# Exponentials kept as 25-bit integers, and their low halves converted on three engines

## The chip, the cores and the metric

The kernel runs on one core of a Trainium2 chip. A core has five engines that run side by side, each through its own list of instructions in order: TensorE (PE; its weight loads are listed as PEld), VectorE (DVE), ScalarE (ACT), GpSimd (POOL) and SyncE (SP, which here only issues DMA transfers). They work on SBUF, the memory on the core with 128 partitions; PE writes its products to PSUM, a small memory that DVE and ACT read. They wait for each other through semaphores.

The metric is the device time of one execution in microseconds (us), as the median of the runs. The time of one instruction is given in nanoseconds (ns) where it is short.

## The reference

Attention over pooled queries, then a mixture of experts on its output. Cut to what matters here:

```python
def _attn_ref(q, k, v):                       # batch 8, heads 8, S 1152, D 64
    q_pool = q.reshape(B, H, S // 2, 2, D).mean(axis=3)
    scores = 1.0 / np.sqrt(D) * np.matmul(q_pool, k.transpose(0, 1, 3, 2))
    scores = scores - np.max(scores, axis=-1, keepdims=True)
    attn = np.exp(scores)
    attn = attn / (np.sum(attn, axis=-1, keepdims=True) + 1e-09)
    return np.matmul(attn, v)

def _moe_ref(x, modality_id, w_gate, modality_bias, w1, w2):   # 4608 tokens, 512, 8 experts, 1024
    logits = x @ w_gate + modality_bias[modality_id]
    e_idx = np.argmax(logits, axis=1)
    ...
    for e in range(E):
        mask = e_idx == e
        h = np.maximum(x[mask] @ w1[e], 0.0)
        out[mask] = gate_w[mask, None] * (h @ w2[e])
```

The experts are chosen by the largest logit, so attention's result is needed with nearly float32 precision: a rounding that changes the order of two logits sends a token to another expert.

## The kernel before

**Stages.** Attention runs over 32 pairs (`npairs`); a pair is one head of two neighbouring batches, so that 2 x 64 dimensions fill the 128 partitions. A pair has 18 steps (`NSTEP`). Its scores are computed in 18 chunks, 9 for each of the two heads (`j`), of 128 keys by 576 queries. The experts follow after the last pair; their routing is worked out beside the attention, in small DVE operations.

**High and low parts.** PE takes 32-bit data at a lower precision than float32, and 16-bit data exactly. So each operand is split into a rounded high part and what is left, and a product is the sum of three matmuls: high x high, high x low, low x high.

**A chunk, in order** (`scores`, lines 717 to 735):

- In two halves of 288 queries, two matmuls each write the scores, minus the row's maximum, to a PSUM tile `psc` of three buffers (lines 729, 730). The maximum comes in as one more row of the operand (`mr`, line 664), which also carries the logarithm of `PSC`, a constant factor on all exponentials.
- ACT takes the exponential to an SBUF tile `Pe` in float32 (line 731).
- The high part `Ph` costs no instruction: it is the upper 16 bits of each float32 of `Pe`, read as bfloat16 with a stride of four bytes.
- The low part `Pl`, in float16, is `Pe - Ph`: one operation with two inputs of 576 elements (line 735), one or two steps later. It runs on POOL, but for the chunks in `DVE_LO` (3 of 18), and for those in `DVE_LAST` (13) in the last pair, which run on DVE.

**Products with v** (`pv`, lines 752 to 765). For each of five groups of queries and each of the nine chunks there are three matmuls, `Ph` x `vh`, `Ph` x `vl` and `Pl` x `vh`, with `Ph` or `Pl` as the weights. `vh` (`VH`, float16, two buffers) is v scaled by a power of two and rounded, made by ACT in three parts (`values`, line 652); `vl` is what is left, made by DVE (line 650). A column of ones beside `vh` gives the sum of the exponentials, by which `evac` divides (lines 772 to 787).

**Beside it, for the next pairs.** DVE takes the row maxima of a first, rough pass over the scores: PE writes 27 tiles `pm` per pair (line 681) and DVE reduces each to one column `mp` (line 682). Keys and queries are split (ACT line 560, DVE lines 547 and 573, POOL line 541), and SP moves the parts into the matmuls' operands `B1`, `B2` and `QB` (line 510). Each pair loads its keys and queries (`load_kq`, line 523) and its values (`load_v`, line 527); the finished output of two pairs is stored by SP (line 197). ACT squares v for its scale (line 618); the scale is a short chain of DVE operations (lines 627 to 639) behind a matmul with a 128 x 128 tile `ones` (line 625).

**What sets the order.** Inside attention the order on PE and ACT is written out by hand: the loop at lines 918 to 948 goes through the steps, and in each of them through the letters of `ORD`. `s` is half a chunk of scores with its exponential, `M` and `X` a tile of the maximum pass, `V` six groups of products with v, and `F` what was put off to this step: `later(n, f)` puts off f by n steps, and `at(t, p, f)` sets it to step t of pair p. The `T_` constants at the top of the file are those steps: `T_VH` for `vh` and `T_VL` for `vl`, for instance. So the low part of an even chunk comes in the step after its exponential, that of an odd chunk in the step after that.

Small SBUF tiles of the routing (`route` and `place`, in pools with one buffer) have a name and a place each.

Of the kernel before, what the change touches and what calls it, by code (L numbers as in the profile page):

```python
# [31 lines left out]
KQ = S + SQ  # L32
NPAIR = BATCH // 2 * H
NKC = S // P
PSC = 64.0
NSTEP = 2 * NKC
NP = 18
T_LIST = -122
# [21 lines left out]
T_POW = 0  # L60
T_VH = (2, 2, 4)
T_VL = (7, 7, 8)
QH_DVE = True
HI_DVE = ()
EV_ACT = ()
# [3 lines left out]
DVE_LAST = (1, 2, 3, 4, 5, 7, 8, 10, 11, 13, 14, 16, 17)  # L69
T_G0 = 2  # L70
T_X0 = 11
DVE_LO = (0, 7, 15)


T = BATCH * SQ
# [59 lines left out]
class Router:  # L135
# [86 lines left out]
    def route(self, g, eng):  # L222

        nc, sm = self.nc, self.sm
        while self.added[g] < H // 2:
            yield 1
        lg = sm.tile([P, NT, E], F32, name="lg8")
        nc.vector.tensor_reduce(lg, self.lg[g].rearrange("p t (w e) -> p t e w", w=3), op=ALU.add, axis=AX.X)
        ts = slice(g * NT, (g + 1) * NT)
        bc = lambda a: a.unsqueeze(2).broadcast_to([P, NT, E])  # L230
        be = lambda a: a.unsqueeze(1).broadcast_to([P, NT, E])
        w = sm.tile([P, NT, E], F32, name="w_a")
        w2 = sm.tile([P, NT, E], F32, name="w_b")
        inv = sm.tile([P, NT], F32, name="inv")
        nc.vector.tensor_scalar(inv, self.mid[:, ts], -1.0, 1.0, op0=ALU.mult, op1=ALU.add)
        nc.vector.tensor_tensor(w, be(self.b0[:, 0]), bc(inv), op=ALU.mult)
        nc.vector.tensor_tensor(w2, be(self.b0[:, 1]), bc(self.mid[:, ts]), op=ALU.mult)
        yield RS
        nc.vector.tensor_tensor(w, w, w2, op=ALU.add)
        nc.vector.tensor_tensor(lg, lg, w, op=ALU.add)  # L240
        yield RS
        mx = sm.tile([P, NT], F32, name="mx")
        nc.vector.tensor_reduce(mx, lg, op=ALU.max, axis=AX.X)
        nc.vector.tensor_tensor(lg, lg, bc(mx), op=ALU.subtract)
        yield RS
        nc.scalar.activation(w, lg, AF.Exp)
        nc.vector.tensor_single_scalar(w2, lg, 0.0, op=ALU.is_ge)
        key = sm.tile([P, NT, E], F32, name="key")
        nc.vector.scalar_tensor_tensor(key, w2, -float(E), be(self.ie), op0=ALU.mult, op1=ALU.add)
        kmin = sm.tile([P, NT], F32, name="kmin")  # L250
        nc.vector.tensor_reduce(kmin, key, op=ALU.min, axis=AX.X)
        yield RS
        oh = sm.tile([P, NT, E], F32, name="oh")
        nc.vector.tensor_tensor(oh, key, bc(kmin), op=ALU.is_equal)
        oh16 = sm.tile([P, NT, E], BF16, name="oh16")
        nc.vector.tensor_copy(oh16, oh)
        nc.vector.tensor_single_scalar(self.exp[:, ts], kmin, float(E), op=ALU.add)
        yield RS
        sx = sm.tile([P, NT], F32, name="sx")
        nc.vector.tensor_reduce(sx, w, op=ALU.add, axis=AX.X)  # L260
        nc.vector.tensor_single_scalar(sx, sx, EPS, op=ALU.add)
        gt = sm.tile([P, NT, 2], F32, name="gt")
        for i in range(2):
            nc.vector.reciprocal(gt[:, :, i], sx)
        eng.dma_start(out=self.xs[g * NT * P:(g + 1) * NT * P, DM:XW].rearrange("(t p) d -> p t d", p=P), in_=gt)
        yield RS
        for _ in range(self.ll - 1):
            yield
        pr = self.pm(4)[:, 0:(NT + 1) * E].rearrange("p (t e) -> p t e", e=E)
        nc.tensor.matmul(pr[:, 0:NT], self.up, oh16, start=True, stop=False, skip_group_check=True)  # L270
        for s in range(NT):
            nc.tensor.matmul(pr[:, s + 1:], self.on, oh16[:, s:s + 1].broadcast_to([P, NT - s, E]), start=False, stop=s == NT - 1,
                             skip_group_check=True)
        pos = sm.tile([P, NT, E], F32, name="posw")
        nc.vector.tensor_tensor(pos, pr[:, 0:NT], be(self.base), op=ALU.add)
        nb = self.keep.tile([P, E], F32, name="base")
        nc.vector.tensor_tensor(nb, pr[:, NT], self.base, op=ALU.add)
        self.base = nb
        yield RS
        nc.vector.tensor_tensor(pos, pos, oh, op=ALU.mult)  # L280
        nc.vector.tensor_reduce(self.pos[:, ts], pos, op=ALU.add, axis=AX.X)
# [81 lines left out]
    def place(self, nt, late):  # L363
# [1 line left out]
        nc, sm = self.nc, self.sm  # L365
        be = lambda a: a.unsqueeze(1).broadcast_to([P, nt, E])
        yield
        oh = sm.tile([P, nt, E], F32, name=f"ohp{nt}")
        nc.vector.tensor_tensor(oh, self.exp[:, 0:nt].unsqueeze(2).broadcast_to([P, nt, E]), be(self.ie), op=ALU.is_equal)
        yield  # L370
        w = sm.tile([P, nt, E], F32, name=f"ohw{nt}")
        new = lambda name: sm.tile([P, NTT], F32, name=name)[:, 0:nt]

        def pick(o, of):
# [106 lines left out]
def attention(tc, ctx, att, ident, npairs, xpool, on_two, on_split, jobs, side, set_pm, started, ahead, hip):  # L481
# [14 lines left out]
    some = lambda i: ps_max.tile([P, 512], F32, name="pm") if i in IN_PM else small()  # L496
    set_pm(some)

    ones = const.tile([P, P], F32, name="ones")
    B2, QB, VH = [], [], []  # L500
    for i in range(2):
        B2.append(const.tile([D + 1, 2 * KQ], F32R, name=f"B2_{i}"))
        QB.append(const.tile([P, 9, P], F32R, name=f"QB_{i}"))
    for i in range(2):
        VH.append(const.tile([P, NKC, 2, D + 2], F16, name=f"VH_{i}"))

    st = {p: {} for p in range(npairs)}

# [112 lines left out]
    def power(p):  # L621

        s = st[p]
        pt = some(1)
        nc.tensor.matmul(pt[:, 0:NSQ], ones, s["ss"], start=True, stop=True)
        sq = sm.tile([P, 1], F32, name="sq", bufs=1)
        nc.vector.tensor_reduce(sq, pt[:, 0:NSQ], op=ALU.add, axis=AX.X)
        half = sm.tile([P, 1], I32, name="half", bufs=1)
        nc.vector.tensor_single_scalar(half, sq.bitcast(I32), 24, op=ALU.logical_shift_right)
        ex = sm.tile([P, 2], I32, name="ex", bufs=1)  # L630
        nc.vector.tensor_scalar(ex[:, 0:1], half, -1.0, 205.0, op0=ALU.mult, op1=ALU.add)
        nc.vector.tensor_scalar(ex[:, 1:2], half, 1.0, 49.0, op0=ALU.mult, op1=ALU.add)
        sc = sm.tile([P, 2], I32, name="sc")
        nc.vector.tensor_single_scalar(sc, ex, 23, op=ALU.logical_shift_left)
        s["sc"], s["isc"] = sc.bitcast(F32)[:, 0:1], sc.bitcast(F32)[:, 1:2]
        if p % 2 == 0:
            s["both"] = xpool.tile([P, 2], F32, name="both", bufs=3)
        r = slice(p % 2 * D, (p % 2 + 1) * D)
        nc.vector.tensor_copy(st[p - p % 2]["both"][r], sc.bitcast(F32)[r])
# [3 lines left out]
    def values(p, i, lo):  # L643

        s = st[p]
        c = slice(3 * i, 3 * i + 3)
        v = flat(s["v"].rearrange("p (c j d) -> p c j d", c=NKC, j=2)[:, c])
        vh = flat(VH[p % 2][:, c, :, 0:D])
        if lo:
            nc.vector.scalar_tensor_tensor(flat(s["vl"][:, c]), v, s["sc"], vh, op0=ALU.mult, op1=ALU.subtract)  # L650
        else:
            nc.scalar.activation(vh, v, AF.Copy, scale=s["sc"])

    def row(p, mp, u0, u1):

# [61 lines left out]
    def scores(p, j, c, n):  # L717
# [1 line left out]
        s = st[p]  # L719
        b1, b2 = s["B1"], B2[p % 2]  # L720
        ks = slice(j * S + c * P, j * S + (c + 1) * P)
        Pe = pP.tile([P, SQ], F32, name="Pe")
        Pl = pP.tile([P, SQ], F16, name="Pl")
        Ph = Pe.bitcast(BF16).rearrange("p (n w) -> p n w", w=2)[:, :, 1]
        s["P", j, c] = (Ph, Pl)
        for t in range(2):
            qs = slice(2 * S + j * SQ + t * 288, 2 * S + j * SQ + (t + 1) * 288)
# [3 lines left out]
            nc.scalar.activation(Pe[:, t * 288:(t + 1) * 288], pt, AF.Exp, scale=1.0 / 16)  # L731
            if t == 0:
                yield
        eng = nc.vector if (j * NKC + c) in (DVE_LAST if p == npairs - 1 else DVE_LO) else nc.gpsimd
        later(n, lambda: eng.tensor_tensor(Pl, Pe, Ph, op=ALU.subtract))  # L735

    def split_x(p, x2):

# [13 lines left out]
    def pv(p, j, x2):  # L752

        s = st[p]
        W = D + 2
        vh, vl = VH[p % 2], s["vl"]
        hs = slice((p % 2) * D, (p % 2 + 1) * D)
        tile_ = lambda: ps_pv.tile([P, 512], F32, name="xp", tag="pv")[:, 0:5 * W].rearrange("p (g w) -> p g w", w=W)

        def products(qs, out):  # L760
            for c in range(NKC):
                Ph, Pl = s["P", j, c]
                nc.tensor.matmul(out, Ph[:, qs], vh[:, c, j, 0:D + 1], start=c == 0, stop=False, skip_group_check=True)  # L763
                nc.tensor.matmul(out[:, 0:D], Ph[:, qs], vl[:, c, j], start=False, stop=False, skip_group_check=True)  # L764
                nc.tensor.matmul(out, Pl[:, qs], vh[:, c, j, 0:D + 1], start=False, stop=c == NKC - 1, skip_group_check=True)  # L765
                yield

        def evac(xp, g0, t0, n):

            rs = sm.tile([P, 5], F32, name="rs")[:, 0:n]  # L770
            rr = sm.tile([P, 5], F32, name="rr")[:, 0:n]
            nc.vector.tensor_scalar(rs, xp[:, g0:g0 + n, D], 1.0, EPS * PSC, op0=ALU.mult, op1=ALU.add)
            nc.vector.reciprocal(rr, rs)
            def done():
                if p % 2:
# [98 lines left out]
    nc.gpsimd.memset(ones, 1.0)  # L874
    for i in range(2):
        nc.gpsimd.memset(VH[i][:, :, :, D:D + 2], 1.0)
    nc.gpsimd.memset(B2[1][D:D + 1, 0:2 * S].bitcast(F32), 1.0)
    mxq.append(maxpass(0, mp0))
    advance(mxq, T_PRE)
# [2 lines left out]
    for p in range(npairs):  # L882
# [21 lines left out]
        go(T_POW + d, power)  # L904
        for i in range(3):
            go(T_VH[i] if p else min(T_VH[i] + d, NKC), values, i, False)
            go(T_VL[i] if p else min(T_VL[i] + d, NKC), values, i, True)
        for j in range(2):
            go(NKC * (j + 1) + LAG, lambda p, j: pvq.append(pv_task(p, j)), j, end=False)
# [442 lines left out]
```

## Time and profile before

| | us |
|---|---|
| median of three runs | 1434.89 |
| lowest and highest run | 1434.81, 1444.65 |
| the profiled execution | 1437.58 |
| its span, first to last instruction | 1435.8 |

The profile is that of one execution. The span is the time from the first to the last instruction on the core, and "busy" is the time in which an engine had an instruction under way. "Granted clock" is the share of full speed at which PE ran. Views of the profile used below:

- **Busy table by stages:** one row for each stretch of time (us from the start), with its length and, for each engine, the busy us and the number of instructions in brackets.
- **Waits:** an engine and line, what it waited for, the us in total, how many times, and the longest. PEld is PE's weight load. SPq is SP's queue of DMA issues.
- **Groups:** line, engine, operation, output <- input with partitions x elements and types, the count; then busy us in all, mean ns of one; then the engine's idle time just before them and what ended it.
- **Durations of one line:** the count, then the smallest, median and largest ns, and when the first and the last began.

### The profile page before, as it was taken

What the parts mean: (1) busy time and instruction counts of PE and PEld (TensorE: products, weight loads), DVE (VectorE), ACT (ScalarE), POOL (GpSimd) and SP (SyncE); (2) the same over time, 40 slices, a digit from 0 to 9 for tenths busy, and PEclk for the clock granted to TensorE, in tenths of its full rate; (3) what the DMA queues carried; (4) which work ended last, traced back from release to release, by engine and by line L of the source; (5) the groups of instructions that cost most, each with busy time, mean ns of one, the idle gap of its engine ahead of it and who ended that gap; (6) DMA issues with size and microseconds to landing.
All of it is one profiled execution on the core that took longest, in us unless ns stands there. A gap on an engine that the chain in (4) does not pass through costs nothing. (4 is left out here: it accounts for less than half of the span.)

```text
span 1435.8 us, 38561 instructions
## 1 busy us (share of the span) xinstructions
PE 1292.6 (90%) x14976; PEld 1181.7 (82%) x14976; DVE 1185.2 (83%) x2233; ACT 868.6 (60%) x2001; POOL 900.5 (63%) x684
## 2 busy tenths in 40 slices
PE   6899999889999988899998888997989899999995
PEld 4788888888888888888887877886879788989894
DVE  6899998889988999889899999956998566566572
ACT  3566776656666665666665556655555566666661
POOL 6667777757777776677775566736444365554642
PEclk9999999989999999999999999999999999999998
DMA  9668788769788786796886868638867778889791
GB/s 230 177 175 196 187 216 193 165 145 208 191 194 187 197 206 147 177 205 183 195 186 161 169 164 178 136 108 230 233 209 245 221 243 256 245 256 274 242 245 41
DMA packets 211284, 280.53 MB, mean 195 GB/s; under 512 B 92816, under 2 KB 150208, under 8 KB 207121
## 3 DMA queue, kind: packets, MB, share of 16 engines
q1 hardware_dynamic: 204960, 258.15, 72.2%
q0 software_dynamic: 6128, 19.78, 4.0%
q8 instruction: 122, 2.00, 0.6%
q14 instruction: 74, 0.60, 0.1%
HBM read 146.11 MB, written 19.18 MB: 115 GB/s over the span
## 5 line engine op out<-in xcount | busy, mean ns | idle before, releaser
L735 POOL TENSOR_TENSOR Pl<-Pe 128x576 f16<-128x576 f32 x470 | 593.3, 1279 | 278.5 <-ACT Pe L731 269.8
L731 ACT ACTIVATE Pe<-psc 128x288 f32<-128x288 f32 x1152 | 432.6, 409 | 293.2 <-PE psc L730 278.4
L682 DVE TENSOR_REDUCE mp<-pm 128x1 f32<-128x384 f32 x832 | 425.5, 542 | 53.0 <-PE pm L681 50.8
L681 PE MATMUL pm<-hi,QB 128*128 128x384 f32 x832 | 321.1, 386 | 59.2 <-DVE mp L682 55.6
L729 PE MATMUL psc<-B 128*128 128x288 f32 x1152 | 350.2, 311 | 19.6 <-ACT Pe L731 18.4
L730 PE MATMUL psc<-B 65*128 65x288 f32 x1152 | 344.4, 306 | 7.4 <-DMA B<-mr 7.4
L763 PE MATMUL xp<-VH,Pe 128*128 128x65 f16 (+1 forms) x2880 | 308.2, 198 | 0.0
L764 PE MATMUL xp<-vl,Pe 128*128 128x64 f16 (+1 forms) x2880 | 304.1, 195 | 0.0
L765 PE MATMUL xp<-VH,Pl 128*128 128x65 f16 (+1 forms) x2880 | 303.2, 195 | 0.9 <-DVE Pl L735 0.9
L763 PEld LDWEIGHTS <-Pe 128*128 128x128 bf16 (+1 forms) x2880 | 271.7, 103 | 27.8 <-issue 11.1
L765 PEld LDWEIGHTS <-Pl 128*128 128x128 f16 (+1 forms) x2880 | 272.0, 102 | 1.1 <-DVE Pl L735 1.1
L764 PEld LDWEIGHTS <-Pe 128*128 128x128 bf16 (+1 forms) x2880 | 272.0, 103 | 0.0
L729 PEld LDWEIGHTS psc<-B 128*128 128x128 f32 x1152 | 228.5, 198 | 35.5 <-ACT Pe L731 34.8
L730 PEld LDWEIGHTS psc<-B 65*128 65x128 f32 x1152 | 226.5, 197 | 10.3 <-DMA B<-mr 5.7
L681 PEld LDWEIGHTS pm<-hi,QB 128*128 128x128 f32 x832 | 164.3, 198 | 74.2 <-DVE mp L682 66.1
L1078 POOL TENSOR_TENSOR w1l<-w1r,w1h 128x1024 fp32r<-128x1024 f32 x36 | 90.2, 2506 | 142.9 <-ACT w1h L1077 142.6
L1093 PE MATMUL ph<-xpart,w1h 128*128 128x256 f32 x544 | 155.6, 286 | 6.6 <-ACT xpart L1049 5.4
L1094 PE MATMUL ph<-xpart,w1h 128*128 128x256 f32 x544 | 155.5, 286 | 6.7 <-DVE xpart L1050 6.6
L1095 PE MATMUL ph<-xpart,w1l 128*128 128x256 f32 x544 | 154.9, 285 | 0.0
L1141 PE MATMUL po<-w2h,hl 128*128 128x512 f32 x296 | 118.2, 399 | 4.3 <-DVE hl L1099 4.3
L1139 PE MATMUL po<-w2h,hh 128*128 128x512 f32 x296 | 118.1, 399 | 0.0
L1140 PE MATMUL po<-w2l,hh 128*128 128x512 f32 x296 | 117.9, 398 | 0.0
(244 smaller groups left out, 2242.9 us busy)
## 6 DMA issues: line engine op xcount, KB each, us to landing
w2r<-in_w_dram SPq DMA_DIRECT2D x76, 512.0 KB
w1r<-in_w_dram SPq DMA_DIRECT2D x75, 512.0 KB
B<-hi SPq DMA_DIRECT2D x128, 288.0 KB
rawkq<-in_att_dram SPq DMA_DIRECT2D x31, 1152.0 KB
B<-qh SPq DMA_DIRECT2D x128, 144.0 KB
B<-rawkq SPq DMA_DIRECT2D x64, 288.0 KB
rawv<-in_att_dram SPq DMA_DIRECT2D x32, 576.0 KB
B<-rawkq SPq DMA_DIRECT2D x64, 144.0 KB
```

The costliest lines, as they stand in the source:

```text
L681: nc.tensor.matmul(pm, QB[p % 2][:, u], s["hi"][:, t * 384:(t + 1) * 384], start=True, stop=True)
L682: nc.vector.tensor_reduce(mp[:, u, t:t + 1], pm, op=ALU.max, axis=AX.X)
L729: nc.tensor.matmul(pt, b1[:, ks], b1[:, qs], start=True, stop=False)
L730: nc.tensor.matmul(pt, b2[:, ks], b2[:, qs], start=False, stop=True)
L731: nc.scalar.activation(Pe[:, t * 288:(t + 1) * 288], pt, AF.Exp, scale=1.0 / 16)
L735: later(n, lambda: eng.tensor_tensor(Pl, Pe, Ph, op=ALU.subtract))
L763: nc.tensor.matmul(out, Ph[:, qs], vh[:, c, j, 0:D + 1], start=c == 0, stop=False, skip_group_check=True)
L764: nc.tensor.matmul(out[:, 0:D], Ph[:, qs], vl[:, c, j], start=False, stop=False, skip_group_check=True)
L765: nc.tensor.matmul(out, Pl[:, qs], vh[:, c, j, 0:D + 1], start=False, stop=c == NKC - 1, skip_group_check=True)
L1093: nc.tensor.matmul(ph[:, f], hi[:, c, fs], xh[:, c], start=c == 0, stop=False)
L1094: nc.tensor.matmul(ph[:, f], hi[:, c, fs], xl[:, c], start=False, stop=False)
L1095: nc.tensor.matmul(ph[:, f], lo[:, c, fs], xh[:, c], start=False, stop=c == 3)
```

## The change

The exponential is written as an integer, and both halves of it are read in place:

- `PSC` becomes 2^25 instead of 64, and `Pe` an int32 tile, so ACT rounds the exponential to an integer of up to 25 bits.
- `Ph` is the upper 16 bits of each integer, at most 512, read as float16: as a bit pattern these are the tiny numbers n x 2^-24.
- `Pl` is the lower 16 bits, read as uint16, times 2^-24 (`LOW`), in float16. That is an operation with one input and a constant instead of one with two inputs.
- In each of the first 31 pairs the 18 of them go to ACT (8 chunks, `LO_ACT`), DVE (2, `LO_DVE`) and POOL (the other 8). In the last pair 13 stay on DVE and 5 on POOL.
- The lower half counts 2^-16 of the upper one. So the third product takes `vs` instead of `vh`: a second copy `VS` of `VH` times 2^-16, two buffers, written by POOL in three parts of 384 elements at the steps `T_VS`.
- For the room that `VS` takes, `ones` becomes one column that is read 128 times, and the routing's tiles of 72 elements share two tiles `wide0` and `wide1` with each other and with those of `place`.

```diff
-PSC = 64.0
+PBITS = 25
+PSC = 2.0 ** PBITS
+LOW = 2.0 ** -24
...
+T_VS = (5, 5, 6)
...
-DVE_LO = (0, 7, 15)
+LO_DVE = (0, 9)
+LO_ACT = (1, 3, 5, 7, 10, 12, 14, 16)
...
-        lg = sm.tile([P, NT, E], F32, name="lg8")
+        big = [sm.tile([P, 3, NT, E], F32, name=f"wide{i}") for i in range(2)]
+        lg = big[0][:, 0]
...
-    ones = const.tile([P, P], F32, name="ones")
+    ones = const.tile([P, 1], F32, name="ones")
...
+        VS.append(const.tile([P, NKC, 2, D + 2], F16, name=f"VS_{i}"))
...
-        nc.tensor.matmul(pt[:, 0:NSQ], ones, s["ss"], start=True, stop=True)
+        nc.tensor.matmul(pt[:, 0:NSQ], ones.broadcast_to([P, P]), s["ss"], start=True, stop=True)
...
+    def shifted(p, i):
+
+        c = slice(3 * i, 3 * i + 3)
+        nc.gpsimd.tensor_single_scalar(flat(VS[p % 2][:, c, :, 0:D]), flat(VH[p % 2][:, c, :, 0:D]), 2.0 ** -16, op=ALU.mult)
...
-        Pe = pP.tile([P, SQ], F32, name="Pe")
+        Pe = pP.tile([P, SQ], I32, name="Pe")
         Pl = pP.tile([P, SQ], F16, name="Pl")
-        Ph = Pe.bitcast(BF16).rearrange("p (n w) -> p n w", w=2)[:, :, 1]
+        word = lambda dt, w: Pe.bitcast(dt).rearrange("p (n w) -> p n w", w=2)[:, :, w]
+        Ph, rest = word(F16, 1), word(U16, 0)
...
-        eng = nc.vector if (j * NKC + c) in (DVE_LAST if p == npairs - 1 else DVE_LO) else nc.gpsimd
-        later(n, lambda: eng.tensor_tensor(Pl, Pe, Ph, op=ALU.subtract))
+        i = j * NKC + c
+        unit = LOW
+        if i in LO_ACT and p < npairs - 1:
+            later(n, lambda: nc.scalar.activation(Pl, rest, AF.Copy, scale=unit))
+        else:
+            eng = nc.vector if i in (DVE_LAST if p == npairs - 1 else LO_DVE) else nc.gpsimd
+            later(n, lambda: eng.tensor_single_scalar(Pl, rest, unit, op=ALU.mult))
...
-                nc.tensor.matmul(out, Pl[:, qs], vh[:, c, j, 0:D + 1], start=False, stop=c == NKC - 1, skip_group_check=True)
+                nc.tensor.matmul(out, Pl[:, qs], vs[:, c, j, 0:D + 1], start=False, stop=c == NKC - 1, skip_group_check=True)
...
+        nc.gpsimd.memset(VS[i][:, :, :, D:D + 2], 2.0 ** -16)
...
+            go(T_VS[i] if p else min(T_VS[i] + d, NKC), shifted, i)
```

The constant that `evac` adds to the sum (line 772) is scaled to match.

More of the change, by code (lines that the diff above doesn't have):

```diff
@@ L231, in route @@
         be = lambda a: a.unsqueeze(1).broadcast_to([P, NT, E])
-        w = sm.tile([P, NT, E], F32, name="w_a")
-        w2 = sm.tile([P, NT, E], F32, name="w_b")
+        w, w2 = big[0][:, 1], big[0][:, 2]
         inv = sm.tile([P, NT], F32, name="inv")
@@ L247, in route @@
         nc.vector.tensor_single_scalar(w2, lg, 0.0, op=ALU.is_ge)
-        key = sm.tile([P, NT, E], F32, name="key")
+        key = big[1][:, 0]
         nc.vector.scalar_tensor_tensor(key, w2, -float(E), be(self.ie), op0=ALU.mult, op1=ALU.add)
@@ L252, in route @@
         yield RS
-        oh = sm.tile([P, NT, E], F32, name="oh")
+        oh = big[1][:, 1]
         nc.vector.tensor_tensor(oh, key, bc(kmin), op=ALU.is_equal)
@@ L273, in route @@
                              skip_group_check=True)
-        pos = sm.tile([P, NT, E], F32, name="posw")
+        pos = big[1][:, 2]
         nc.vector.tensor_tensor(pos, pr[:, 0:NT], be(self.base), op=ALU.add)
@@ L367, in place @@
         yield
-        oh = sm.tile([P, nt, E], F32, name=f"ohp{nt}")
+        wide = lambda i: sm.tile([P, nt, E], F32, name=f"ohp{nt}_{i}") if late else sm.tile([P, 3, NT, E], F32, name=f"wide{i}").rearrange("p q t e -> p (q t) e")
+        oh = wide(0)
         nc.vector.tensor_tensor(oh, self.exp[:, 0:nt].unsqueeze(2).broadcast_to([P, nt, E]), be(self.ie), op=ALU.is_equal)
         yield
-        w = sm.tile([P, nt, E], F32, name=f"ohw{nt}")
+        w = wide(1)
         new = lambda name: sm.tile([P, NTT], F32, name=name)[:, 0:nt]
@@ L497, in attention @@
     set_pm(some)
-    ones = const.tile([P, P], F32, name="ones")
-    B2, QB, VH = [], [], []
+    ones = const.tile([P, 1], F32, name="ones")
+    B2, QB, VH, VS = [], [], [], []
     for i in range(2):
@@ L755, in pv @@
         W = D + 2
-        vh, vl = VH[p % 2], s["vl"]
+        vh, vs, vl = VH[p % 2], VS[p % 2], s["vl"]
         hs = slice((p % 2) * D, (p % 2 + 1) * D)
@@ L771, in evac @@
             rr = sm.tile([P, 5], F32, name="rr")[:, 0:n]
-            nc.vector.tensor_scalar(rs, xp[:, g0:g0 + n, D], 1.0, EPS * PSC, op0=ALU.mult, op1=ALU.add)
+            nc.vector.tensor_scalar(rs, xp[:, g0:g0 + n, D], 1.0, EPS * PSC * LOW / 2 ** 16, op0=ALU.mult, op1=ALU.add)
             nc.vector.reciprocal(rr, rs)
```

## The prediction

> **What bounds the kernel now.** I read the page's first part, then the busy table by stages, then the waits of the longest stage, then its groups of instructions.
>
> ```profile
> PE 1292.6 (90%) x14976; PEld 1181.7 (82%) x14976; DVE 1185.2 (83%) x2233; ACT 868.6 (60%) x2001; POOL 900.5 (63%) x684
> ```
> ```profile
> core 0: us, PE busy (x) PEld busy (x) DVE busy (x) ACT busy (x) POOL busy (x), PEclk, DMA share, GB/s
> 75.00:925.00 850.00, 767.51 (x11157) 712.56 (x11155) 789.36 (x1662) 543.35 (x1501) 603.24 (x468) 0.97 0.78 182
> ...
> 650.00:675.00 25.00, 24.53 (x386) 22.99 (x385) 24.11 (x50) 18.16 (x51) 20.83 (x16) 1.00 0.69 181
> ...
> 282.00:283.00 1.00, 0.00 (x0) 0.00 (x0) 1.00 (x4) 0.53 (x3) 0.34 (x1) 1.00 1.68 119
> ...
> 288.00:289.00 1.00, 1.00 (x6) 1.00 (x6) 0.56 (x1) 0.67 (x2) 0.00 (x0) 0.50 1.00 187
> ```
> The reader is to see that the averages of the page hide a stage: in the 850 us of steady attention DVE is busy 789 (93%) and PE 768 (90%), ACT 543 (64%), POOL 603 (71%). The change touches this stage alone, apart from its ends. PE has three losses there. It idles 82.5 us. It runs at a mean granted clock of 0.97, so 3% of 850, 25.5 us, is lost to stretches at half clock, and they come after a stop (PE idle at 282, clock 0.50 at 288). And its matmuls are not dense when they wait on each other's readers. In the undisturbed 25 us from 650 the clock is full and both engines are nearly saturated.
>
> ```profile
> ACT Pe L731 <- PE psc L730: 249.2, 252, 3.7
> ...
> PE pm L681 <- DVE mp L682: 50.6, 57, 3.7
> ...
> ACT vl L618 <- DMA rawv<-in_att_dram: 23.7, 13, 2.9
> ...
> PE psc L729 <- ACT Pe L731: 15.1, 13, 2.1
> ...
> PE psc L730 <- DMA B<-mr: 5.0, 7, 1.5
> ...
> PE pm L214 <- DVE mp L682: 4.2, 10, 0.4
> ...
> PE pm L681 <- DVE mr L664: 2.4, 3, 1.1
> ```
> ```profile
> SPq L197 <- DVE m L658: 101.0, 13, 8.2
> ...
> SPq L527 <- DVE vl L650: 53.3, 17, 13.1
> ```
> PE's longest wait is for DVE to empty the maximum tiles (50.6 + 4.2 + 2.4 = 57 us). The load of v (L527) stands in SP's queue behind work that waits for DVE: the rawv buffer's last reader L650 and the x store L197. A late rawv then stops ACT (23.7), which stops PE (15.1). So DVE ends last, directly and through SP, and ACT has 307 us of idle time, mostly waiting for PE.
>
> **What DVE loses to POOL.** First the groups of this stage, then the smallest, median and largest single duration of those lines over the whole run.
>
> ```profile
> L735 POOL TENSOR_TENSOR Pl<-Pe 128x576 f16<-128x576 f32 x439 | 554.9, 1280 | 248.8 <-ACT Pe L731 240.3 <-ACT w_a L246 6.9 <-DMA rawv<-in_att_dram 0.5
> ...
> L731 ACT ACTIVATE Pe<-psc 128x288 f32<-128x288 f32 x1051 | 395.2, 409 | 263.3 <-PE psc L730 249.2 <-POOL Pl L735 5.9 <-PE pm L681 5.1
> ...
> L650 DVE SCALAR_TENSOR_TENSOR vl<-rawv,sc,VH 128x384 f16<-128x384 f32 x88 | 87.2, 1014 | 0.0
> L735 DVE TENSOR_TENSOR Pl<-Pe 128x576 f16<-128x576 f32 x87 | 79.5, 914 | 6.4 <-ACT Pe L731 4.1
> ...
> L573 DVE TENSOR_TENSOR rawkq<-rawkq,hi 128x576 f32<-128x576 f32 x58 | 56.8, 979 | 0.0
> ...
> L541 POOL TENSOR_TENSOR rawkq<-rawkq 128x576 f32<-128x576 f32 x28 | 50.9, 1818 | 0.0
> ...
> L639 DVE COPY both<-sc 64x2 f32<-64x2 f32 x29 | 28.0, 965 | 0.5
> ...
> L634 DVE TENSOR_SCALAR sc<-ex 128x2 int32<-128x2 int32 x29 | 22.2, 764 | 0.0
> ```
> ```profile
> L735 POOL TENSOR_TENSOR Pl<-Pe x470: 1137/1147/2027, 24.5 to 958.6; 128x576 f16<-128x576 f32 x157
> L650 DVE SCALAR_TENSOR_TENSOR vl<-rawv,sc,VH x96: 597/1030/1746, 43.5 to 944.1; 128x384 f16<-128x384 f32 x96
> L573 DVE TENSOR_TENSOR rawkq<-rawkq,hi x60: 737/745/1697, 58.4 to 897.5; 128x576 f32<-128x576 f32 x60
> L639 DVE COPY both<-sc x32: 148/1000/1109, 40.3 to 937.2; 64x2 f32<-64x2 f32 x32
> L634 DVE TENSOR_SCALAR sc<-ex x32: 162/804/1103, 39.5 to 937.0; 128x2 int32<-128x2 int32 x32
> L547 DVE CAST qh<-rawkq x30: 442/447/895, 50.0 to 884.9; 128x576 fp32r<-128x576 f32 x30
> ```
> A copy of two elements takes 148 ns at best and 1000 in the median: about one POOL subtraction (1147) stands in its time. The excess of mean over smallest, times count, is 88 x 0.417 = 36.7 (L650), 58 x 0.242 = 14.0 (L573), 29 x 0.817 = 23.7 (L639) and 29 x 0.602 = 17.5 (L634): 92 us of DVE's 789, beside what is in its own 87 subtractions.
>
> **The change, part by part.** 1051 exponentials at 36 a pair are 29.2 pairs in this stage, 29.1 us each.
>
> Pl on DVE: 87 two-input operations (79.5 us) become 58 one-input ones. Nearest is L547, same width, one input: 0.447. The ends are 0.44 and the 0.914 it replaces; with some waiting I take 0.50, 29 us: DVE -50.
>
> Pl on POOL goes from 15 to 8 a pair, and three VS multiplies of 384 elements come. Rows for one-input work on POOL are small:
>
> ```profile
> L192 POOL CAST part<-io x1: 187/187/187, 21.6 to 21.6; 128x1 f32<-128x1 int32 x1
> ...
> L192 POOL CAST col<-io x1: 215/215/215, 22.6 to 22.6; 128x38 f32<-128x38 int32 x1
> ```
> The slope, 28 ns over 37 elements, gives 187 + 576 x 0.76 = 0.62 us; the other end is the two-input 1.15. I take 0.80 nearer to the one-input rows, and 0.62 for a VS (0.48 to 0.83). POOL per pair: 8 x 0.80 + 3 x 0.62 + 1.82 (L541) = 10.1, times 29.2 = 294 us instead of 603. That halves the 92 us: DVE -45. DVE would be busy 789 - 95 = 694, or 23.8 us a pair. VS is issued at step 5 of a pair and first read after step 10, so it hides.
>
> The Trainium skill (GPSIMD Engine Reference, sections 1 and 4.1) says that POOL shares its SBUF interfaces with VectorE and collides with two-input operations and with two-port fast ones; the L639 row, 148 against 1000, agrees. By that rule DVE's faster Pl collides as the old one did, and a Pl near 0.9 would leave 23 us less of DVE's gain.
>
> Pl on ACT, new: 8 a pair, 233 in the stage.
>
> ```profile
> L549 ACT CAST qh<-rawkq 128x576 fp32r<-128x576 f32 x1 | 0.7, 671 | 4.0 <-DMA B<-qh 4.0
> ```
> That is 0.671 each, 156 us: ACT goes to 699, 23.9 us a pair. In ACT's order the next exponentials queue behind them, and PE's score tiles (three buffers) behind those. The cover is the 249 us in which ACT waits for psc, about 1 us on each of 252 occasions. Bounds on what PE pays are 0 and 156; I take 15, because the occasions outnumber the 233 operations and are longer, but four squares and three VH lie in the same steps.
>
> A page speaks against this placing: the Trainium skill (ScalarE: Activation LUTs, Rules for kernel authors) sends multiplies to VectorE. By it the eight would run on DVE, 233 x 0.447 = 104 us, and DVE would be back at 798 with nothing won; the trace is against it, with 307 us idle on ACT and 61 on DVE.
>
> Nothing for the rest: the exponential writes 4 bytes as before, weight loads of Ph keep their stride, the shared router tiles are used by one chain of DVE work in order, and the `ones` weight is loaded twice a pair. If these covers fail it is some tenths of a us a pair, 10 us at most by my estimate from 29 pairs.
>
> Sum: of the 57 us that PE waits for DVE, 48 go, as DVE falls from 27.0 to 23.8 us a pair against about 25 of PE work (the stretch from 650); of the 25.5 us of clock two thirds, 17, since their stops come from late DVE, mr and rawv; of the 5.0 for mr, 4; ACT gives back 15; the stretches before 75 and after 925, 115 us with the same operations, give 8. That is -62, 27.3 us a pair. The profiled execution was 1437.6 (span 1435.8), 2.7 above the median of the runs: 1437.6 - 62 - 2.7 = **1373**. With DVE's waits all gone or half gone, two thirds to none of the clock's rest, and ACT at 0 to 40, this case spans 1345 to 1405.
>
> **Rivals.** (1) ACT becomes the bound, and the kernel is slower. A Pl stands between exponentials; should each cost PE 0.42 us, 233 x 0.42 = 98 against the 77 won, the time is 1437.6 - 2.7 + 21 = 1456. It decides from 0.33 us each. For it: 23.9 us a pair is close to the 25 of PE, and rawv waits would come on top. Against: the 249 us.
> (2) Full relief: PE reaches the 25.0 us of the stretch from 650 in nearly all pairs; 29.2 x 25.2 = 736, -114 and -8 outside, less the 2.7: 1313; with half of the difference, 1343.
> (3) POOL's one-input form is no cheaper (1.15): POOL then works 8 x 1.15 + 3 x 0.83 + 1.82 = 13.5 a pair, 394 us, the contention falls by a third (-31), DVE's Pl stays near 0.9 (-27), and PE gets half: 1405 to 1415.
> (4) The change doesn't do what it says: PE's hand-written order, not DVE, sets the pace, and only mishaps move. 1425 to 1440.
>
> **How the numbers follow.** Forecast 0.58, rival 1 0.12, rival 2 0.13, rival 3 0.10, rival 4 0.07. About 1% is what a measurement can tell from no change: under 1420.5 is faster, over 1449 slower. Faster: 0.58 + 0.13 + 0.09 = 0.80; same 0.08; slower 0.12. The range 1325 to 1425 leaves out rival 1, most of rival 4 and the far end of rival 2, under 0.2.
>
> **What would show it.** Right: PE pm <- DVE mp falls from 50.6 to 15 or less, L639's median from 1000 to half, POOL's busy time near 300 in the stage, fewer half-clock stretches, ACT near 24 us a pair. Wrong: PE psc <- ACT Pe well above 40 us (rival 1), Pl on POOL above 1.1 us (rival 3), or DVE's busy time down while PE's idle time stays (rival 4).

## The result, and the profile after

| | before | after |
|---|---|---|
| median of the runs, us | 1436.43 (4 runs) | 1355.66 (4 runs) |
| lowest, highest | 1434.81, 1444.65 | 1350.83, 1368.26 |
| profiled execution, us | 1437.58 | 1359.31 |
| its span, us | 1435.8 | 1357.6 |

The ratio of the runs is 0.944, with a 95% interval of 0.936 to 0.952: 81 us less, of which the forecast had 62. The median of before has one run more than it had for the prediction.

The first part of the page, of after:

```profile
PE 1266.3 (93%) x14976; PEld 1167.9 (86%) x14976; DVE 1058.4 (78%) x2202; ACT 985.0 (73%) x2249; POOL 848.1 (62%) x565
```

The busy table by stages, over the steady part of attention. It is shorter now, so the stage is taken from 75 to 845 us:

```profile
core 0: us, PE busy (x) PEld busy (x) DVE busy (x) ACT busy (x) POOL busy (x), PEclk, DMA share, GB/s
...
75.00:845.00 770.00, 738.46 (x11047) 697.28 (x11046) 669.19 (x1616) 647.97 (x1720) 543.08 (x348) 0.98 0.86 199
```

The groups of that stage:

```profile
L752 POOL TENSOR_SCALAR Pl<-Pe 128x576 f16<-128x576 uint16 x232 | 403.3, 1739 | 226.2 <-ACT Pe L743 220.9 <-DMA rawkq<-in_att_dram 2.5 <-ACT wide L250 1.1
L743 ACT ACTIVATE Pe<-psc 128x288 int32<-128x288 f32 x1040 | 390.7, 410 | 100.3 <-PE psc L742 93.5 <-PE pm L692 0.8
...
L749 ACT ACTIVATE Pl<-Pe 128x576 f16<-128x576 uint16 x231 | 157.1, 680 | 0.0
...
L663 POOL TENSOR_SCALAR VS<-VH 128x384 f16<-128x384 f16 x87 | 105.9, 1228 | 0.3
L656 DVE SCALAR_TENSOR_TENSOR vl<-rawv,sc,VH 128x384 f16<-128x384 f32 x87 | 69.5, 824 | 0.9 <-ACT VH L658 0.9
...
L752 DVE TENSOR_SCALAR Pl<-Pe 128x576 f16<-128x576 uint16 x57 | 26.2, 460 | 3.5 <-ACT Pe L743 2.6
...
L645 DVE COPY both<-sc 64x2 f32<-64x2 f32 x29 | 8.2, 283 | 0.4
```

The 1040 exponentials are 28.9 pairs, 26.7 us each instead of 29.1. In 28.9 pairs that is 71 of the 78 us between the two profiled executions. DVE's work fell from 27.0 to 23.2 us a pair. But POOL, whose work was to halve, is busy 543 of 770 us, 71% as before: its one-input low part takes 1.74 us, more than the two-input one it replaces (1.28).

The waits of the same stage:

```profile
ACT Pe L743 <- PE psc L742: 93.5, 169, 2.4
...
ACT vl L624 <- DMA rawv<-in_att_dram: 22.3, 14, 2.4
PE psc L741 <- ACT Pe L743: 19.7, 14, 2.2
...
PE pm L692 <- DVE mp L693: 4.3, 11, 0.7
...
PE psc L742 <- DMA B<-mr: 1.8, 3, 1.1
...
PE pm L692 <- DVE mr L675: 1.1, 2, 0.9
```

PE's wait for DVE's maximum tiles is gone (50.6 to 4.3). The late load of v still stops ACT, and ACT PE. The durations of single lines over the whole run say why DVE has room although POOL is as busy as it was:

```profile
L752 POOL TENSOR_SCALAR Pl<-Pe x253: 1642/1651/2846, 29.9 to 876.8; 128x576 f16<-128x576 uint16 x127
L645 DVE COPY both<-sc x32: 151/221/602, 40.6 to 858.4; 64x2 f32<-64x2 f32 x32
L656 DVE SCALAR_TENSOR_TENSOR vl<-rawv,sc,VH x96: 601/855/1115, 42.6 to 863.1; 128x384 f16<-128x384 f32 x96
```

The copy of two elements takes 221 ns in the median, where it took 1000. POOL's median is close to its smallest value (1651 and 1642), so at least half of its operations are not held up either. The question for the experiments was what DVE's waits depend on, if not on how much POOL works.

### The profile page after: what moved, and what is told of

The parts are those of the page before. It is cut to its first block, busy times and chain, and to the rows that moved or that the text cites. A ratio compares the mean times of both kernels' runs of the same rounds, so it can differ in the third digit from the quotient of the medians.

```text
span 1357.6 us, 38150 instructions
## 1 busy us (share of the span) xinstructions
PE 1266.3 (93%) x14976; PEld 1167.9 (86%) x14976; DVE 1058.4 (78%) x2202; ACT 985.0 (73%) x2249; POOL 848.1 (62%) x565
## 5 line engine op out<-in xcount | busy, mean ns | idle before, releaser
L752 POOL TENSOR_SCALAR Pl<-Pe 128x576 f16<-128x576 uint16 x253 | 439.1, 1736 | 251.0 <-ACT Pe L743 245.7
L743 ACT ACTIVATE Pe<-psc 128x288 int32<-128x288 f32 x1152 | 431.8, 410 | 116.1 <-PE psc L742 108.7
L741 PE MATMUL psc<-B 128*128 128x288 f32 x1152 | 344.1, 306 | 24.5 <-ACT Pe L743 24.1
L692 PE MATMUL pm<-hi,QB 128*128 128x384 f32 x832 | 316.3, 380 | 6.8 <-DVE mp L693 4.5
L780 PE MATMUL xp<-VH,Pe 128*128 128x65 f16 (+1 forms) x2880 | 302.8, 197 | 0.0
L782 PE MATMUL xp<-VS,Pl 128*128 128x65 f16 (+1 forms) x2880 | 298.1, 194 | 1.1 <-POOL VS L663 0.7
L781 PE MATMUL xp<-vl,Pe 128*128 128x64 f16 (+1 forms) x2880 | 299.0, 194 | 0.0
L780 PEld LDWEIGHTS <-Pe 128*128 128x128 f16 (+1 forms) x2880 | 268.2, 102 | 27.9 <-issue 11.3
L781 PEld LDWEIGHTS <-Pe 128*128 128x128 f16 (+1 forms) x2880 | 268.5, 102 | 0.0
L741 PEld LDWEIGHTS psc<-B 128*128 128x128 f32 x1152 | 225.1, 195 | 34.7 <-ACT Pe L743 33.3
L749 ACT ACTIVATE Pl<-Pe 128x576 f16<-128x576 uint16 x248 | 168.7, 680 | 0.0
L663 POOL TENSOR_SCALAR VS<-VH 128x384 f16<-128x384 f16 x96 | 117.4, 1233 | 2.0 <-ACT VH L658 1.7
```

What stands on the lines that cost most here:

```text
L692: nc.tensor.matmul(pm, QB[p % 2][:, u], s["hi"][:, t * 384:(t + 1) * 384], start=True, stop=True)
L741: nc.tensor.matmul(pt, b1[:, ks], b1[:, qs], start=True, stop=False)
L749: later(n, lambda: nc.scalar.activation(Pl, rest, AF.Copy, scale=unit))
L752: later(n, lambda: eng.tensor_single_scalar(Pl, rest, unit, op=ALU.mult))
L782: nc.tensor.matmul(out, Pl[:, qs], vs[:, c, j, 0:D + 1], start=False, stop=c == NKC - 1, skip_group_check=True)
```

## The experiments

Theories: by the **form theory**, an operation with two tensor inputs on POOL holds up DVE and one with a single input hardly does. By the **number** and **busy-time theories** the count of POOL's operations, or the share of time in which POOL works, decides. Ratios are to the kernel before on the same chip, since that kernel took from 1429 to 1441 us in the median on the chips used.

### The form undone, the counts kept

```diff
-            later(n, lambda: eng.tensor_single_scalar(Pl, rest, unit, op=ALU.mult))
+            if eng is nc.gpsimd and p < npairs - 1:
+                later(n, lambda: eng.tensor_tensor(Pl, Pe.bitcast(F32), word(BF16, 1), op=ALU.subtract))
+            else:
+                later(n, lambda: eng.tensor_single_scalar(Pl, rest, unit, op=ALU.mult))
```

> The changed kernel, with POOL's 8 low parts a pair back in the old two-input form (float32 minus its upper half, which gives zero here: the low part of these 8 chunks is left out). Counts and places stay. Form theory (a two-input operation on POOL holds up DVE's operations, a one-input one hardly does): the two-element copy goes from a median of 221 ns back to 700 or more, the vl operation from 812 to 900 or more on average, though POOL's operations get shorter (1.65 to about 1.2 us) and its busy time falls by some 100 us; time 1375 to 1400. Number theory (DVE's waits fell because POOL has fewer operations, 12 a pair for 16): the copy stays under 300 ns, time 1345 to 1360.

1379.3 us, ratio 0.957 (0.951 to 0.963). The busy table of the stage, then durations and groups of the whole run:

```profile
75.00:845.00 770.00, 722.74 (x10700) 679.50 (x10699) 677.64 (x1568) 629.42 (x1669) 445.33 (x337) 0.97 0.84 194
```
```profile
L645 DVE COPY both<-sc x32: 147/693/798, 39.0 to 881.3; 64x2 f32<-64x2 f32 x32
```
```profile
L753 POOL TENSOR_TENSOR Pl<-Pe 128x576 f16<-128x576 f32 x248 | 313.5, 1264 | 344.4 <-ACT Pe L743 332.5 <-DMA rawkq<-in_att_dram 6.8 <-ACT wide L250 5.1
...
L656 DVE SCALAR_TENSOR_TENSOR vl<-rawv,sc,VH 128x384 f16<-128x384 f32 x96 | 91.0, 972 | 0.4 <-ACT VH L658 0.4
```

POOL's low part is shorter (1.26 us), POOL works less, and yet DVE's copy goes from 221 to 693 ns in the median, its vl operation from 812 to 972 on average, and the time up. The number theory falls: the counts are the same.

But the time rose by only 1.1 to 1.3% of the kernel before (0.957, for the 0.944 and, in a later run, 0.946 of the changed kernel). With POOL's old form the change still gives 4.3%: in this stage DVE works 24.2 us a pair (27.0 before, 23.2 in the changed kernel), and PE's wait for the maximum tiles is 17.5 us (46.5 in the same 770 us before, 4.3 after). Of the 2.8 us a pair that DVE works less than before, 1.8 are its own low parts (79.5 us in the stage before, 26.3 here), which are fewer here too and in the new form.

### The form alone, in the kernel before

```diff
-        later(n, lambda: eng.tensor_tensor(Pl, Pe, Ph, op=ALU.subtract))
+        rest = Pe.bitcast(U16).rearrange("p (n w) -> p n w", w=2)[:, :, 0]
+        if eng is nc.gpsimd:
+            later(n, lambda: eng.tensor_single_scalar(Pl, rest, 2.0 ** -24, op=ALU.mult))
+        else:
+            later(n, lambda: eng.tensor_tensor(Pl, Pe, Ph, op=ALU.subtract))
```

> The kernel before, with only POOL's 15 low parts a pair in the one-input form (lower 16 bits times a constant, which isn't the low part, so the result is less exact). POOL's busy time rises, from 71% to about 90% of the attention stage. Form theory: DVE's waits go all the same, the two-element copy from 1000 ns to under 300 and the vl operation from 1014 to about 800; DVE gains some 80 us and the time falls to 1380 to 1410, less than that only if POOL at 26 us a pair becomes the bound. Busy-time theory (as the prediction had it, DVE waits in proportion to POOL's busy time): the copy stays at 1000 ns or goes above, time 1435 to 1480.

1373.0 us, ratio 0.954 (0.948 to 0.960). Its busy table, durations and one wait:

```profile
75.00:845.00 770.00, 723.30 (x10877) 678.14 (x10874) 698.78 (x1617) 532.86 (x1467) 766.56 (x458) 1.00 0.84 196
```
```profile
L639 DVE COPY both<-sc x32: 151/592/703, 41.2 to 871.4; 64x2 f32<-64x2 f32 x32
L650 DVE SCALAR_TENSOR_TENSOR vl<-rawv,sc,VH x96: 601/610/1080, 44.2 to 876.4; 128x384 f16<-128x384 f32 x96
```
```profile
PE xp L769 <- POOL Pl L737: 22.0, 30, 1.1
```

POOL works without a pause, 766.6 of 770 us, and DVE is held up less than before: the vl operation's median falls from 1030 to 610 ns. The busy-time theory, which was the prediction's, falls. The copy falls to 592, not under 300: some wait is left when POOL never stops. The time is a little below the range expected. This one line, alone, gives 4.6%, although it has PE waiting 22 us for POOL; the rest of the change without it gave 4.3% (the run above). The two gains don't add up: together they are 5.6%.

### POOL's forms, by themselves

A kernel of nine stretches: POOL runs one form 20 times, and DVE meanwhile the same 22 operations. The forms, and what DVE runs beside each:

```
                                                            line
nc.gpsimd.tensor_tensor(lo, pe, hi, op=ALU.subtract)        173
nc.gpsimd.tensor_single_scalar(lo, half, UNIT, op=ALU.mult) 184   uint16, every second one
nc.gpsimd.tensor_single_scalar(lo, dense, UNIT, ...)        195   uint16, dense
nc.gpsimd.tensor_single_scalar(res, pe, UNIT, ...)          206   float32 to float32
nc.gpsimd.tensor_single_scalar(lo, pe, UNIT, ...)           217   float32 to float16
nc.gpsimd.tensor_copy(lo, half)                             228
nc.gpsimd.tensor_tensor(lo, pe, units.broadcast_to(...))    239
nc.gpsimd.tensor_tensor(res, pe, pe2, op=ALU.add)           250
for _ in range(10): nc.vector.tensor_copy(both[0:64], tiny[0:64])
for _ in range(6):  nc.vector.scalar_tensor_tensor(vc, va, units, vb, ...)
for _ in range(6):  nc.vector.tensor_single_scalar(pl, low, UNIT, op=ALU.mult)
```

> No attention and no experts: the output is left zero. Nine stretches; in each POOL runs one form 20 times (none in the first) while DVE runs ten two-element copies, six operations with two inputs of 384 and six one-input low parts of 576. Form theory: the copy takes about 150 ns in the first stretch, about 1000 on average beside any of the three two-input forms, and 600 or less beside any of the one-input forms, whatever their own length. For POOL's own duration: if the 16-bit strided input is what makes it slow, the strided uint16 form takes 1.65 us and the dense or float32 one under 1.0; if the one-input form with a constant is slow as such, all of those take 1.4 us or more and only the plain copy less. Rival to the form theory (what counts is how long POOL's operation is): the copy's time follows POOL's duration from stretch to stretch.

The groups, as the view sorts them: POOL's forms first, then DVE's `vc` operation and its copy. DVE's copy stands two lines behind the form beside which it runs and its `vc` operation four: 175 and 177 beside the two-input form of 173, 186 and 188 beside the multiply of 184, 230 beside the cast of 228, 252 beside the addition of 250. 164 and 166 run with POOL idle.

```profile
L206 POOL TENSOR_SCALAR res<-pe 128x576 f32<-128x576 f32 x20 | 33.3, 1667 | 1.6
L184 POOL TENSOR_SCALAR lo<-pe 128x576 f16<-128x576 uint16 x20 | 33.3, 1667 | 1.6
...
L250 POOL TENSOR_TENSOR res<-pe,pe 128x576 f32<-128x576 f32 x20 | 29.7, 1483 | 1.5
L173 POOL TENSOR_TENSOR lo<-pe 128x576 f16<-128x576 f32 x20 | 24.6, 1232 | 1.5
...
L228 POOL CAST lo<-pe 128x576 f16<-128x576 uint16 x20 | 15.2, 762 | 1.2
...
L177 DVE SCALAR_TENSOR_TENSOR vc<-va,units,vb 128x384 f16<-128x384 f32 x6 | 8.4, 1403 | 0.2
...
L252 DVE COPY both<-tiny 64x2 f32<-64x2 f32 x10 | 7.0, 704 | 0.3
L175 DVE COPY both<-tiny 64x2 f32<-64x2 f32 x10 | 5.9, 588 | 0.3
...
L188 DVE SCALAR_TENSOR_TENSOR vc<-va,units,vb 128x384 f16<-128x384 f32 x6 | 5.0, 827 | 0.2
...
L166 DVE SCALAR_TENSOR_TENSOR vc<-va,units,vb 128x384 f16<-128x384 f32 x6 | 3.7, 616 | 0.2
L230 DVE COPY both<-tiny 64x2 f32<-64x2 f32 x10 | 3.4, 337 | 0.3
L186 DVE COPY both<-tiny 64x2 f32<-64x2 f32 x10 | 3.1, 314 | 0.3
...
L164 DVE COPY both<-tiny 64x2 f32<-64x2 f32 x10 | 1.6, 159 | 0.3
```

The copy takes 159 ns alone, 588 and 704 beside a two-input form, 314 beside the multiply and 337 beside the cast. The multiply is the longest of POOL's operations (1667) and the cast the shortest (762), with nearly the same effect on DVE; so from form to form the wait doesn't follow POOL's duration. Between the two-input forms it does grow with it (588 beside 1232, 704 beside 1483). The 1000 ns expected beside two inputs was too much here. And the multiply's length is that of the form: with dense, strided, 16-bit and 32-bit inputs it took the same 1667 ns.

### ACT's eight low parts elsewhere

To POOL (`LO_ACT = ()`), and to DVE:

```diff
-LO_DVE = (0, 9)
-LO_ACT = (1, 3, 5, 7, 10, 12, 14, 16)
+LO_DVE = (0, 1, 3, 5, 7, 9, 10, 12, 14, 16)
+LO_ACT = ()
```

> The changed kernel with the 8 low parts of ACT given to POOL, 16 a pair. Theory: ACT's part is needed since POOL's one-input operation is slow (1.65 us): 16 x 1.65 + 3 x 1.17 + 1.42 = 31.3 us a pair against a period of 26.7, so POOL is the bound and the time is 1480 to 1510. Rival (ACT's 248 operations cost PE time, as rival 1 of the prediction, and POOL's 251 us of waiting take up more): time 1330 to 1355.

> The changed kernel with the 8 low parts of ACT given to DVE, 10 a pair there. Theory (DVE and PE are both close to the bound): DVE's 23.2 us a pair grow by 8 x 0.46 = 3.7 to 26.9, above the period of 26.7; PE's wait for the maximum tiles rises from 4 to 30 us or more; time 1375 to 1415. Rule for multiplies (VectorE rather than ScalarE) and the rival that ACT holds up PE: PE's wait for ACT falls from 20 us to under 5 and the time is 1335 to 1355.

POOL: 1511.1 us, ratio 1.050 (1.043 to 1.056). DVE: 1384.5, ratio 0.960 (0.954 to 0.967). One wait of the first over its whole run and its busy table, then two waits of the second over its whole run:

```profile
PE xp L782 <- POOL Pl L752: 117.9, 90, 2.5
```
```profile
75.00:845.00 770.00, 665.68 (x9269) 627.18 (x9268) 573.41 (x1317) 455.79 (x1248) 769.13 (x491) 0.91 0.71 170
```
```profile
PE pm L692 <- DVE mp L693: 30.3, 28, 3.2
...
PE psc L741 <- ACT Pe L743: 4.3, 3, 3.8
```

Without ACT, POOL works 769 of 770 us and PE waits for it: the kernel would be slower than before, by a microsecond more than the range expected. With the eight on DVE, PE's wait for the maximum tiles comes back (30.3 us over the whole run, for 4.5 in the changed kernel's), and the wait for ACT that goes in exchange (24.1 to 4.3, over the same) is worth less. The rule for multiplies, weighed in the prediction (the Trainium skill, ScalarE: Activation LUTs, Rules for kernel authors), loses here to the measurement.

### What ACT still costs: fewer low parts, and the late v

```diff
-LO_ACT = (1, 3, 5, 7, 10, 12, 14, 16)
+LO_ACT = (1, 3, 5, 7, 10, 12)
```

> The changed kernel with two of ACT's 8 low parts, chunks 14 and 16 (the steps where ACT also squares v), given to POOL: 10 there, 21.4 us a pair. If ACT still holds up PE (PE waits 20 us for exponentials), that wait falls to 12 or less and the time to 1340 to 1350; if those waits come from the late load of v and not from ACT's load, the wait stays near 20 and the time is 1353 to 1368.

1345.8 us, but the kernel before took 1429.0 on that chip: the ratio is 0.943 (0.940 to 0.946), that of the change itself. In the stage, PE's wait for exponentials fell from 19.7 to 7.0 us, though ACT still waited 16.8 us for v; the time did not follow beyond the noise:

```profile
ACT vl L624 <- DMA rawv<-in_att_dram: 16.8, 14, 1.9
...
PE psc L741 <- ACT Pe L743: 7.0, 12, 1.1
```

The other place to look is SP's queue. In the changed kernel the store waits for DVE there, over the whole run:

```profile
SPq L201 <- DVE Pl L752: 79.2, 13, 6.5
```

```diff
                 if p % 2:
-                    on_two(p // 2, x2)
+                if p % 2 and p < npairs - 1:
+                    later_end(1, lambda: on_two(p // 2, x2))
+                elif p % 2:
+                    on_two(p // 2, x2)
```

> The changed kernel with the store of the finished output put behind the load of the next v on SP's queue, in all pairs but the last. If the load stands behind the store's wait for DVE, ACT's wait for v (22 us in the attention stage) falls under 8, PE's wait for exponentials from 20 to 10 or less, and the time to 1335 to 1348. If the load is late because of the transfers themselves, nothing moves: 1350 to 1362.

1324.8 us, ratio 0.929 (0.925 to 0.933), less than the range expected. In the stage, ACT's wait for v is gone, PE waits 0.9 us for exponentials, and PE is busy 98%:

```profile
75.00:845.00 770.00, 755.35 (x11575) 712.45 (x11574) 688.61 (x1671) 672.64 (x1793) 564.06 (x361) 1.00 0.83 203
```
```profile
PE psc L741 <- ACT Pe L743: 0.9, 4, 0.3
```

The same store behind the load in the kernel before:

> The kernel before with the store behind the load of v, and nothing else. If DVE bounds that kernel, the earlier load frees ACT (24 us of waiting) but DVE's 93% stay, and the time falls by 5 to 20 us: 1415 to 1430. If the late v and not DVE was what held it up, it falls as in the changed kernel, by 30 us or more: 1400 or less.

1405.6 us, ratio 0.975 (0.970 to 0.979). That lies between the two ranges expected; the 36 us less (1440.6 for the kernel before on that chip) are those of the second answer. There PE's wait for DVE's maximum tiles stays at 47.6 us (46.5 in the same 770 us before), while ACT no longer waits for v:

```profile
PE pm L681 <- DVE mp L682: 47.6, 51, 3.7
```

So two things held up the kernel before, DVE and, apart from it, the load of v behind the store.

### The best version

Both edits of the last part together, once more beside the changed kernel on one chip:

> The changed kernel with both: six low parts on ACT and the store behind the load of v. With the store moved, PE was busy 755 of 770 us in the attention stage. If PE is now the bound, relieving ACT adds nearly nothing: 1318 to 1327. If ACT still sets the pace at times, the two gains (10 and 31 us) add in part: 1308 to 1317.

> The changed kernel itself, on one chip with the next two, since the kernel before took 1429 us on one chip and 1440 on another. Its ratio to the kernel before should again be 0.944, in 0.936 to 0.952.

> The store behind the load of v, as in the run above, now beside the changed kernel: 0.98 to 0.99 of its time if the 0.929 and 0.944 of the runs before hold.

> Store moved and six low parts on ACT. If PE is the bound once the store is moved, it is within 0.3% of the run before it; if ACT still cost something there, it is 0.4% or more below it.

Both together: 1332.1 us, ratio 0.924 (0.920 to 0.929), where the kernel before took 1440.6. In us that is above both ranges expected, which were set by the run of the moved store, on a chip where the kernel before took 1429.0. On one chip, with 1439.7 before: the changed kernel 1360.2, ratio 0.946 (0.943 to 0.950); with the store moved 1328.0, ratio 0.922 (0.919 to 0.924); with both 1330.7, ratio 0.924 (0.922 to 0.926). Moving the store takes 2.4% off the changed kernel, more than the 1 to 2% expected, and beats both kernels; relieving ACT on top adds nothing that can be told, as expected if PE is the bound.

## Why the prediction was right, and which of its steps was not

**DVE and PE's wait for it.** Right: the wait for DVE was to lose 48 us. Counted with PE's transposes that wait for the maxima (2.4 us before, 3.2 after), it was some 60 us in the stage and is some 9. DVE's work a pair came to 23.2 us, for 23.8 forecast.

**The low part on DVE.** Right: 79.5 to 26.2 us in the stage, -53 for -50. It runs at 460 ns, near the 447 of the cast that was taken for it. That the collision which the prediction weighed (a Pl near 0.9) didn't come rests on the order, of which the prediction said nothing: in the stretch of the trace that was looked at (340 to 395 us) each of the five low parts on DVE ran while POOL stood idle. By themselves, in the kernel of POOL's forms, such operations took 459 ns with POOL idle, 790 beside its multiply and 1302 beside the two-input form of line 173.

**POOL's price.** Wrong. "I take 0.80 nearer to the one-input rows, and 0.62 for a VS": they took 1.74 and 1.23, outside both ends (0.62 to 1.15 and 0.48 to 0.83). The rows were casts; the cast costs about what their slope says (0.66 us at its smallest, over the same 576 elements), but the multiply 1.65. The Trainium skill (GPSIMD Engine Reference, section 4.1) has one-input operations at roughly line rate; the cast agrees with it, at (662 - 187) / 576 = 0.82 ns an element, and the multiply, at 2.5, does not.

**"That halves the 92 us".** The step that failed: it let DVE's waits follow POOL's busy time. POOL's share stayed at 71%, and by that step nothing would have been won here. Rival 3, "POOL's one-input form is no cheaper", came nearest on the price (it put it at 1.15 us, and 1.74 was measured), and said 1405 to 1415 for it. Yet the excess over the smallest duration fell from 92 to about 28 us (L656 87 x 0.223 = 19.4, L579 58 x 0.072 = 4.2, L645 29 x 0.132 = 3.8, L640 0.3), -64 for the -45 of the forecast. The forecast came out through two errors of opposite sign, the price of POOL's operations and what their busy time does to DVE, and a little too small for it. That this term had the right sign was luck.

What stands in its place can be worked out by the same sum from the first two experiments. POOL's two-input operations are those of the low part and the one of line 541 (547 in the changed kernel):

| kernel | POOL busy in the stage | POOL's two-input operations a pair | excess on DVE, us |
|---|---|---|---|
| before | 71% | 16 | 92 |
| the form undone, the counts kept | 58% | 9 | 59 |
| the form alone, in the kernel before | 100% | 1 | 32 |
| changed | 71% | 1 | 28 |

The 59 are 33.3 for the vl operation, 10.0 for that on the keys, 14.5 for the copy and 0.9 for the shift (L640); the 32 are 10.8, 5.6, 10.6 and 4.6. So DVE's waits followed how much two-input work POOL had, not how much it worked. Both the new form and the sharing out of the low parts lower it, which fits that the two gains don't add up. This is an account of four kernels; no run varied that number by itself.

**ACT.** The eight low parts cost 680 ns for 671, and ACT's work a pair 22.4 us for 23.9. PE's wait for exponentials rose by 4.6 us, for 15. Rival 1 fell. Of the 19.7 us that are left, the moved store took away all but 0.9 with ACT's eight low parts in place, and two low parts fewer all but 7.0 with v still late. So the late v and ACT's load make that wait together.

**The late v.** The prediction had it as DVE's doing ("DVE ends last, directly and through SP"). With DVE relieved it stayed, 23.7 us before and 22.3 after; moving the store ended it. It was the place of the load in the queue, a second limit that the prediction had seen in the rows and gave no term of its own, beyond its share of the clock.

**The clock.** -17 was forecast; the stretches at half clock fell from 51 to 31 us in this stage, -10 us at full speed. They belong for the most part to the stops that the late v still causes: six of the seven such stretches begin within 9 us behind a stop of 1.4 to 2.2 us in which PE waited for ACT and ACT for v, and with the store moved the granted clock of the stage is 1.00. The size varies from one execution to the next: in the one profiled for the comparison on one chip, the changed kernel had 10 us at half clock.

**The sum.** -51 for the waits, -10 for the clock, -3 for mr, +5 for ACT are -59; the stage gave -71. The other 12 are in PE's busy time, which fell from 26.3 to 25.6 us a pair, more than the clock explains; that was not in the sum, and no run shows what shortened it. Outside the stage it is -7, for -8.

## What to carry to other kernels

Where two engines hold each other up, look at the form of their operations and count those of the form that collides, not the busy time: here a longer operation on POOL freed DVE, since it has one input. Price an operation by a row of the same operation; a cast is no stand-in for a multiply. And when an engine stops for a load, look at what stands ahead of that load on its queue: a store that waits for its data was worth 2.4%.

## What the runs showed of the hardware

- On POOL a multiply by a constant took 1.65 us for 576 elements whatever its types and stride, a cast 0.66 and a two-input operation 1.15 to 1.39 at their smallest. POOL's two-input operations held up DVE's copies and two-input operations far more than its one-input ones: 580 to 704 ns against 313 to 337 for a copy of 159, and 1403 to 1656 against 827 to 920 for a two-input operation of 616. What in POOL makes the difference is not shown by any run.
- Halves of an integer read as float16, down to the tiniest numbers, cost PE nothing: 196 ns a matmul before and after, 100 and 99 ns a weight load.
- A wait that the profile lists in full need not be worth its length: PE's wait for exponentials fell by 13 us with two low parts fewer on ACT, and the ratio to the kernel before only from 0.944 or 0.946 (two measurements of the changed kernel) to 0.943, which is within the noise.
